# Windowed attention and two expert layers on one core: the first pass of the first layer in the attention's list, q and k in rows of 96 tokens

## The chip, the core and the metric

The kernel runs on one core of one Trainium2 chip, in one launch. The metric is the device time in microseconds (us). The engines are named as in the profile: PE is TensorE (matmul), PEld its weight loads, DVE is VectorE, ACT is ScalarE, POOL is GpSimd, SP is SyncE, which only issues DMAs here.

## What is computed

Attention with a window of 128 tokens over 4 batches, 8 heads, 576 tokens and 64 columns a head; its output, 2304 tokens of 512 columns, goes through two expert layers (512 to 2048 to 512).

```python
rel = pos[:, None] - pos[None, :]
slopes = 2.0 ** (-8.0 * (np.arange(H) + 1) / H)
scores = q @ k.T / np.sqrt(D) + slopes * -abs(rel)      # where 0 <= rel < 128, else -1e9
attn = softmax(scores) @ v                              # sum + 1e-9
x = attn.transpose(0, 2, 1, 3).reshape(B * S, H * D)    # 2304 x 512
h = x @ w_in                                            # first layer
P = a[0] + a[1] * h + a[2] * h**2 + a[3] * h**3
Q = 1.0 + abs(b[0]) * abs(h) + abs(b[1]) * h**2
x = (P / (Q + 1e-6)) @ w_out
h = x @ w2_in                                           # second layer
out = where(h > 0, h, exp(min(h, 0)) - 1) @ w2_out
```

The weights come as 64-bit floats, and the kernel makes 32-bit ones of them on the chip.

## The kernel before

**Attention.** There are 16 units: a batch and a pair of heads. For each unit q, k and v are loaded; q and k come as four tiles of 128 tokens and one of 64 (three DMAs each, the last tile padded with zeros). TensorE transposes them (`qT`, `kT`: five blocks of 128 columns each), ScalarE copies q's (`qC`) and VectorE k's transposes (`kC`) from PSUM, and VectorE the last 64 tokens of both (`zC`). Then come the scores `S` in two halves, nine tiles `t` of 64 queries by up to 192 keys for both heads; VectorE adds the bias and takes the minimum (`D`, L615), ScalarE takes the exponential and the row sums (`E`, L621), VectorE the inverse of the sums in two parts (`R`, L629 and L630: five tiles, then four), GpSimd multiplies the probabilities by it (`N`, L633), TensorE transposes them in four pairs (`T`, L645), ScalarE copies them (`C`, L557), TensorE multiplies by v in two halves (`V`, L675, into the PSUM tiles `evens` and `odds`), and ScalarE copies both results into `xT` (`XE` and `XO`, L557). The probabilities and the raw q, k and v have two sets of buffers each.

**Weights.** A weight tile (there are 32: `wi` and `wo` for 16 blocks of 128 columns of the hidden layer) is loaded as words and takes five steps: scale on ScalarE (`cs`, L279), shift on VectorE (`ca`, L287), join on VectorE (`cb`, L297), high half (`ch`, L305), low half (`cl`, L311). TensorE multiplies halves in three passes: high by high, low by high, high by low.

**First layer.** The 2304 tokens are six blocks `j` of 384. A chunk is a block and one of the 16 hidden blocks `f`: 96 chunks, 16 to a pass. A chunk is GEMM1 (`g`, L402, 12 matmuls into one PSUM bank `h`), the rational function and GEMM2 (`G`, L769, 12 matmuls, added up in four banks over a pass). The rational function has a first part (six operations of ScalarE L445 to L465, three of VectorE) and a second: the high half of the quotient `hi` (L458), the product back (L470), the remainder (L475), and the low half (L476, on VectorE for the first chunks, else on GpSimd).

**What sets the order.** `attention_steps` lists the steps of the attention with engine, cost and needs, `in_time` plays them through with the ranks of the table `OFF`, and `attention` issues them in that order. The list also holds 28 weight conversions, the split of block 0 of x into high and low halves (`xh`, `xl`), GEMM1 of chunks 0 to 3 and the first part of the rational function for chunks 0 and 1. All else is issued by the loop in `experts`: for s from 0 to 95 it issues GEMM1 of chunk s, GEMM2 of chunk s − 3 and `rational(s)`, which is the first part of chunk s and the second part of chunk s − 1; the last four weights are converted on the way (`conv_step`). In the first pass the scale of a weight goes ahead of the GEMMs of every other s. The loop then goes on into the second layer, which is not touched.

Of the kernel before, what the change touches and what calls it, by code (L numbers as in the profile page):

```python
# [41 lines left out]
def attention_steps():  # L42
# [75 lines left out]
    for c in range(4):
        gone = [("S", 14, m) for m in range(2)] if c == 0 else [("S", 15, m) for m in range(2)]
        gone += [("D", 15, t) for t in range(9)] if c == 3 else []  # L120
        step(("xh", c), "ACT", 415, ("XE", 12), ("XO", 12), *gone)
        step(("xl", c), "DVE", 470, ("xh", c))
        bank = {0: ("kC", 15)}.get(c)
        free = [bank] if bank else [("D", 15, t) for t in range(9)]
        for kk in range(4):
            step(("g", c, kk), "PE", 520, ("xl", kk), ("cl", 2 * c), *free, ("g", c, kk - 1),
                 *([("g", c - 1, 3)] if kk == 0 else []))
    for c in range(2):
        gone = [("b_abs",), ("r", c - 1, 3), *[(x, 15, t) for t in range(9) for x in "DN"]]
        step(("r", c, 0), "ACT", 1750, ("g", c, 3), *(gone if c else gone[:2]))  # L130
        step(("r", c, 1), "DVE", 475, ("r", c, 0))
        step(("r", c, 2), "ACT", 900, ("r", c, 1))
# [1213 lines left out]
```

## Time and profile before

| | us |
|---|---|
| median of 3 runs | 939.21 (939.2 to 939.39) |
| profiled execution | 937.85 |
| its span, first to last instruction | 936.1 |
| TensorE busy | 906.1 (97%) |
| VectorE busy | 783.4 (84%) |
| ScalarE busy | 731.6 (78%) |
| GpSimd busy | 178.7 (19%) |

The profile is of one execution. Times are counted from the start of its span, in us; durations of groups are means in ns. "Idle before" is the time an engine stood still ahead of an instruction, and the name behind the arrow is what it waited for. The granted clock (PEclk) is the share of its full speed that the chip let TensorE run at. The stage of the attention ends at about 150 us, the first layer at about 550, the second fills the rest.

### The profile page before, as it was taken

How to read it: one execution, taken by the hardware profiler on the slowest of the kernel's cores; microseconds unless marked ns; L12 is line 12 of the kernel's file. 1: busy time of each engine (PE TensorE's matmuls, PEld its weight loads, DVE VectorE, ACT ScalarE, POOL GpSimd, SP SyncE). 2: the span in 40 equal slices, each digit the busy share in tenths (PEclk: the TensorE clock that was granted, in tenths of full speed). 3: DMA queues.
4: the chain of work that ended last, by engine and by line, in shares of the span. 5: the costliest groups of instructions: out<-in, count | busy, mean ns of one | idle time of the engine just before them, and what ended most of it. 6: DMA issues, size and time to landing. Idle time of an engine off the chain costs nothing.

```text
span 936.1 us, 18028 instructions
## 1 busy us (share of the span) xinstructions
PE 906.1 (97%) x6148; PEld 834.2 (89%) x6148; DVE 783.4 (84%) x1851; ACT 731.6 (78%) x1635; POOL 178.7 (19%) x264
## 2 busy tenths in 40 slices
PE   7989987999999999999999989999999999999998
PEld 4766666999999999999999978898988888888887
DVE  6988997998998998988989979998968688777653
ACT  5999997988898888889888968676867567766553
POOL 4566561122222222222222210000000000000000
PEclk8999998999999999999999989999999999999999
DMA  7999962011222222222200124445243423442201
GB/s 172 220 219 219 242 191 76 1 35 60 83 79 74 87 61 91 85 63 87 84 31 28 46 73 142 150 144 186 92 158 106 124 79 99 150 147 79 80 1 67
DMA packets 112428, 98.43 MB, mean 105 GB/s; under 512 B 62800, under 2 KB 86096, under 8 KB 112336
## 3 DMA queue, kind: packets, MB, share of 16 engines
q1 hardware_dynamic: 109936, 96.70, 34.8%
q8 instruction: 48, 0.79, 0.4%
q10 hardware_dynamic: 2400, 0.59, 0.3%
q14 instruction: 44, 0.36, 0.1%
HBM read 79.96 MB, written 17.30 MB: 104 GB/s over the span
## 4 chain that ended last, share of the span: by engine, by line
PE 76%; DVE 5%; ACT 2%; issue 1%; POOL 0%; DVEq 0%; ACTq 0%
PE acc L993 21%; PE acc L769 19%; PE m L977 19%; PE h L402 18%; DVE ghi L458 1%; DVE ee L479 1%; DVE qq L461 1%; DVE ee L475 1%; DVE qq L470 1%; DVE h L478 0%; ACT rr L464 0%; ACT rr L465 0%; DVE xo_wo L934 0%; DVE xo_wi L934 0%; DVE t_wi L955 0%
## 5 line engine op out<-in xcount | busy, mean ns | idle before, releaser
L402 PE MATMUL h<-xs,w_wi 128*128 128x384 f32 x1152 | 218.3, 336 | 0.0
L402 PEld LDWEIGHTS h<-xs,w_wi 128*128 128x128 f32 x1152 | 201.0, 188 | 0.3
L769 PE MATMUL acc<-ghi,w_wo 128*128 128x384 f32 x768 | 197.3, 338 | 3.0 <-DVE ghi L458 3.0
L476 POOL TENSOR_TENSOR glo<-ee,rr 128x384 fp32r<-128x384 f32 x92 | 93.7, 1018 | 313.3 <-DVE ee L475 106.3
L769 PEld LDWEIGHTS acc<-ghi,w_wo 128*128 128x128 f32 x768 | 140.4, 190 | 3.4 <-DVE ghi L458 3.4
L769 PE MATMUL acc<-glo,w_wo 128*128 128x384 f32 x384 | 129.6, 337 | 0.8 <-DVE glo L476 0.8
L993 PE MATMUL acc<-op_wo,ghi 128*128 128x512 f32 x288 | 89.6, 392 | 0.0
L977 PE MATMUL m<-xo_wi,op_wi 128*128 128x384 f32 x336 | 77.2, 337 | 0.0
L977 PE MATMUL m<-xo_wo,op_wi 128*128 128x384 f32 x336 | 76.5, 335 | 0.2 <-ACT oo L1043 0.2
L769 PEld LDWEIGHTS acc<-glo,w_wo 128*128 128x128 f32 x384 | 73.0, 190 | 1.3 <-DVE glo L476 1.3
L1039 ACT ACTIVATE oo<-qq 128x384 f32<-128x384 f32 x24 | 12.6, 523 | 77.0 <-DVE qq L1033 77.0
L464 ACT ACTIVATE rr<-qq,c_q 128x384 f32<-128x384 f32 x94 | 57.8, 615 | 15.0 <-DVE qq L461 14.2
L447 ACT ACTIVATE oo<-h,a_sb 128x384 f32<-128x384 f32 x94 | 66.4, 706 | 2.3 <-DVE h L478 2.0
L461 DVE SCALAR_TENSOR_TENSOR qq<-h,b_abs,qa 128x384 f32<-128x384 f32 x92 | 56.1, 609 | 14.0 <-ACT qa L446 12.9
L450 ACT ACTIVATE ee<-h,a_sb 128x384 f32<-128x384 f32 x94 | 66.1, 703 | 0.0
L977 PEld LDWEIGHTS m<-xo_wo,op_wi 128*128 128x128 f32 x336 | 60.8, 188 | 4.4 <-ACT oo L1043 0.4
L458 DVE TENSOR_TENSOR ghi<-ee,rr 128x384 fp32r<-128x384 f32 x96 | 53.5, 557 | 12.2 <-ACT h L445 0.5
L993 PEld LDWEIGHTS acc<-op_wo,ghi 128*128 128x128 f32 x288 | 53.5, 188 | 8.9
L479 DVE TENSOR_TENSOR ee<-ee,h 128x384 f32<-128x384 f32 x94 | 52.2, 555 | 10.2 <-DVE h L478 0.5
L977 PEld LDWEIGHTS m<-xo_wi,op_wi 128*128 128x128 f32 x336 | 60.5, 188 | 0.0
L445 ACT ACTIVATE h<-h 128x384 f32<-128x384 f32 x94 | 45.4, 483 | 16.6 <-PE h L402 16.0
L1033 DVE TENSOR_TENSOR ee<-ee,m 128x384 f32<-128x384 f32 x96 | 52.7, 549 | 5.8 <-PE m L977 5.5
(198 smaller groups left out, 2064.4 us busy)
## 6 DMA issues: line engine op xcount, KB each, us to landing
pair<-joined_wo SPq DMA_DIRECT2D x43, 256.0 KB, 2.7
raw_wo<-in_moe_w_out_dram SPq DMA_DIRECT2D x20, 512.0 KB, 4.1
raw_wi<-in_moe_w_in_dram SPq DMA_DIRECT2D x16, 512.0 KB, 4.3
half<-in_moe_w_in_dram SPq DMA_DIRECT2D x32, 256.0 KB, 2.7
two_wo<-joined_wi SPq DMA_DIRECT2D x32, 256.0 KB, 2.8
s<-sums SPq DMA_DIRECT2D x32, 256.0 KB, 2.8
half<-in_moe_w_out_dram SPq DMA_DIRECT2D x22, 256.0 KB, 2.8
v<-in_v_dram SPq DMA_DIRECT2D x32, 128.0 KB, 3.9
```

The costliest lines, as they stand in the source:

```text
L402: nc.tensor.matmul(h, lhsT=WT["wi", f][:, SEL[wp], kk * P:(kk + 1) * P], rhs=x[xp][kk], start=(kk == 0 and n == 0), stop=(kk == KD - 1 and ...
L447: nc.scalar.activation(out=oo, in_=h2, func=AF.Identity, scale=a_sb[:, 3:4], bias=a_sb[:, 1:2])
L450: nc.scalar.activation(out=ee, in_=h2, func=AF.Identity, scale=a_sb[:, 2:3], bias=a_sb[:, 0:1])
L458: nc.vector.tensor_tensor(out=hi, in0=ee0, in1=rr0, op=ALU.mult)
L461: nc.vector.scalar_tensor_tensor(out=qq, in0=h2, scalar=b_abs[:, 1:2], in1=qa, op0=ALU.mult, op1=ALU.add)
L464: nc.scalar.activation(out=rr, in_=qq, func=AF.Ln, bias=c_q)
L476: (nc.gpsimd if c > 4 else nc.vector).tensor_tensor(out=low, in0=ee0, in1=rr0, op=ALU.mult)
L479: nc.vector.tensor_tensor(out=ee, in0=ee, in1=h, op=ALU.add)
L769: nc.tensor.matmul(acc_t[d], lhsT=WT["wo", f][:, SEL[wp], d * P:(d + 1) * P], rhs=gt[SEL[xp]], start=(f == 0 and n == 0), stop=(f == KF - ...
L977: nc.tensor.matmul(out, lhsT=w[:, SEL[wp], c0:c0 + P], rhs=XO[q // NP2, nm, k][:, SEL[xp]], start=(k == 0 and n == 0), stop=(k == 1 and n ...
L993: nc.tensor.matmul(acc_t[T, t], lhsT=gt[SEL[xp]][:, t * P:(t + 1) * P], rhs=w[:, SEL[wp]], start=(first and n == 0), stop=(last and n == 2),)
L1033: nc.vector.tensor_tensor(out=t, in0=R[q, x], in1=M[q, m], op=ALU.add)
```

## The change

The function `attention` becomes `attention_and_first_pass`, and its list of steps now holds the whole first pass: all 32 weights, the split of x for blocks 0 and 1, GEMM1 of all 16 chunks in quarters (`g`), the rational function in single operations (`sq` to `lo`), and GEMM2 of chunks 0 to 12 in quarters (`G`). The loop in `experts` starts at s = 16, and the two first `load_half` stand ahead of it. The first 24 weights are converted as before; the last eight, whose slots hold q, k and the probabilities in the attention, come behind it, with the high half on ScalarE. Three of them wait for G of chunks 0 to 2, whose quotients lie in their slots. From chunk 3 on the low half of the quotient is made by GpSimd.

Beside that, q and k come as six tiles of 96 tokens in two DMAs each, without padding: six transposes of 96 columns, copies `qC` and `kC` of 480 columns, `zC` of two times 96. One `R` per unit inverts all nine sums, behind all nine `E`; every `N` waits for it. The copy `XO` is VectorE's. Costs in the list and the table `OFF` have other numbers.

```diff
-MODE = {"qT": 0, "kT": 0, "T": 0, "S": 1, "V": 2}
+CT = 4160
+MODE = {"qT": 0, "kT": 0, "T": 0, "S": 1, "V": 2, "g": 0, "G": 0}
...
-    "ldq": -37303, "ldk": -40037, "ldv": -7307, "qT": 49228, "qC": -19956, "kT": -37687, "kC":
...
+    "ldq": -23769, "ldk": -74006, "ldv": -1434, "qT": 61759, "qC": -31032, "kT": -8967, "kC":
...
-    for key, cost in (("consts", 1000), ("ident", 700), ("rel", 2100), ("rel_t", 2100)):
+    for key, cost in (("ident", 700), ("rel", 1850), ("rel_t", 1850), ("consts", 500)):
...
-            step(("ld", nm, u), "SP", 1550, (nm + "T", u - 2))
-        step(("ld", "v", u), "SP", 1550, ("V", u - 2, 1))
-        step(("qT", u), "PE", 590, ("ld", "q", u), ("ident",), ("consts",), ("kC", u - 1), ("zC", u - 1))
-        step(("kT", u), "PE", 590, ("ld", "k", u), ("ident",), ("consts",), *([("qC", u)] if u else []))
+            step(("ld", nm, u), "SP", 1150, (nm + "T", u - 2))
+        step(("ld", "v", u), "SP", 1700, ("V", u - 2, 1))
+        step(("qT", u), "PE", 550, ("ld", "q", u), ("ident",), ("kC", u - 1), ("zC", u - 1))
...
-            step(("N", u, t), "POOL", {64: 330, 128: 400, 192: 480}[c], ("R", u, int(t > 4)), ("E", u, t))
-        step(("R", u, 0), "DVE", 320, *[("E", u, t) for t in range(5)])
-        step(("R", u, 1), "DVE", 320, *[("E", u, t) for t in range(5, 9)])
+            step(("N", u, t), "POOL", {64: 380, 128: 480, 192: 600}[c], ("R", u), ("E", u, t))
+        step(("R", u), "DVE", 330, *[("E", u, t) for t in range(9)])
...
-        step(("XO", u), "ACT", 264, ("V", u, 0), ("V", u, 1))
+        step(("XO", u), "DVE", 336, ("V", u, 0), ("V", u, 1))
...
+        gone = [("ldw", n - 1)] if n < EARLY else []
+        if n == 22:
+            gone.append(("bias", 3))
+        if EARLY <= n < EARLY + 3:
+            gone += [("G", n - EARLY, d) for d in range(4)]
+        if n == EARLY + 3:
+            gone.append(("kT", 15))
+        if n >= EARLY + 4:
+            v, x = divmod(n - EARLY - 4, 2)
+            gone += [("T", 14 + v, m) for m in ((0, 1), (2, 3))[x]]
+        step(("ldw", n), "SP", 1300, *gone)
+        step(("cs", n), "ACT", 575, ("ldw", n), ("cl", n - 3), ("cs", n - 1))
+        step(("ca", n), "DVE", 340, ("ldw", n))
+        step(("cb", n), "DVE", 590, ("cs", n), ("ca", n))
+        step(("ch", n), *(("DVE", 337) if n < EARLY else ("ACT", 520)), ("cb", n))
+        step(("cl", n), "DVE", 610, ("ch", n))
+    step(("small",), "SP", 300)
+    step(("b_abs",), "ACT", 60, ("small",))
+    over = [("C", 15, m) for m in range(4)] + [("XE", 15), ("XO", 15)]
+    banks = [[(x, 15, t) for x in "D" for t in range(9)]] * 3 + [[("kC", 15), ("qC", 15)]]
...
+    for c in range(16):
+        bank = (3, 0, 1, 2)[c] if c < 4 else (3, 0, 1)[(c - 4) % 3]
+        gone, banks[bank] = banks[bank], [("hm", c)]
+        for kk in range(4):
+            step(("g", c, kk), "PE", 520, ("xl", 0, kk), ("cl", 2 * c), *gone, ("g", c, kk - 1), ("g", c - 1, 3))
+        start = [(x, 15, t) for x in "DN" for t in range(9)] if c == 1 else []
+        step(("sq", c), "ACT", 389, ("g", c, 3), ("oo", c - 1), ("ee", c - 1), ("qq", c - 1), *start)
...
+        gone = [(("qT", 14),), (("qT", 15),), (("kT", 14),), (*over, ("V", 15, 1))][min(c, 3)]
+        step(("hi", c), "DVE", 475, ("ex", c), ("ea", c), *gone, ("G", c - 3, 3))
+        step(("q2", c), "DVE", 588, ("hi", c))
+        step(("e2", c), "DVE", 475, ("q2", c))
+        step(("lo", c), *(("POOL", 1050) if c > 2 else ("DVE", 475)), ("e2", c))
+        for d in range(4 if c < 13 else 0):
+            step(("G", c, d), "PE", 520, ("hi", c), ("lo", c), ("cl", 2 * c + 1), ("G", c, d - 1), ("G", c - 1, 3),
+                 *(over if c == 0 else []))
...
-        if eng == "D":
+        if key in LATE:
+            nc.scalar.activation(out=w[:, 0], in_=T32[key], func=AF.Copy)
+        else:
             nc.vector.tensor_copy(w[:, 0], T32[key])
...
+    def low_quotient(c):
+        _, ee, _, _, rr = r_t.pop(c)
+        (nc.gpsimd if c > 2 else nc.vector).tensor_tensor(out=g_t[c][1], in0=ee, in1=rr, op=ALU.mult)
...
-            shape = [P, NF + 1, 2, D]
+            R6 = S // 6
             whole = {
-                nm: [place(LATE["qk".index(nm) * 2 + n], shape, F32, nm) for n in range(2)] for nm in "qk"
+                nm: [place(LATE["qk".index(nm) * 2 + n], [P, 6, 2, D], F32, nm) for n in range(2)] for nm in "qk"
             }
-            whole["v"] = [raw.tile(shape, F32, name=f"v{n}") for n in range(2)]
+            whole["v"] = [raw.tile([P, NF + 1, 2, D], F32, name=f"v{n}") for n in range(2)]
             units = [(b, p) for p in range(NP) for b in range(B)]
...
-                    eng.dma_start(
-                        out=t[:, 0:NF, e, :],
-                        in_=src[b, 2 * p + e, 0:NF * P, :].rearrange("(t p) d -> p t d", p=P),
-                    )
-                eng.dma_start(
-                    out=t[0:TL, NF, :, :], in_=src[b, 2 * p:2 * p + 2, NF * P:S, :].rearrange("h p d -> p h d")
-                )
+                    if nm == "v":
+                        eng.dma_start(
+                            out=t[:, 0:NF, e], in_=src[e, 0:NF * P].rearrange("(t p) d -> p t d", p=P)
+                        )
+                    else:
+                        eng.dma_start(out=t[0:R6, :, e], in_=src[e].rearrange("(t p) d -> p t d", p=R6))
+                if nm == "v":
+                    eng.dma_start(out=t[0:TL, NF], in_=src[:, NF * P:S].rearrange("h p d -> p h d"))
...
-                    tp_ps[u, n] = ps = bank(1 if (u, n) == (0, 1) else 7, [P, NF, P], "ps_qk")
-                    for i in range(NF + 1):
+                    tp_ps[u, n] = ps = bank(1 if (u, n) == (0, 1) else 7, [P, 5, R6], "ps_qk")
+                    for i in range(6):
                         nc.tensor.transpose(
-                            ps[:, i] if i < NF else odds[:, NF + 2 * n:NF + 2 * n + 2].rearrange("p t c -> p (t c)"),
-                            r[:, i].rearrange("p e d -> p (e d)"), ident,
+                            ps[:, i] if i < 5 else ends[:, n], r[0:R6, i].rearrange("p e d -> p (e d)"),
+                            ident[0:R6, 0:R6],
                         )
                 return run
 
             def q_copy(n, eng):
...
-            def inverse(u, half):
-                t0, t1 = ((0, 5), (5, 9))[half]
-                total = stat(u, 1, t0, t1)
+            def inverse(u):
+                total = stat(u, 1, 0, 9)
                 nc.vector.tensor_scalar(out=total, in0=total, scalar1=1e-9, scalar2=None, op0=ALU.add)
-                nc.vector.reciprocal(out=stat(u, 2, t0, t1), in_=total)
+                nc.vector.reciprocal(out=stat(u, 2, 0, 9), in_=total)
 
...
-                    copy("ACT", x[:, n::2], odds[:, 0:NF] if n else x_t.pop(u))
+                    copy("DVE" if n else "ACT", x[:, n::2], odds[:, 0:NF] if n else x_t.pop(u))
...
-        for s in range(NCH):
+        _, ee, qq, _, rr = r_t.pop(KF - 1)
+        q_t[KF - 1] = (qq, ee, rr)
+        load_half(0)
+        load_half(1)
+        for s in range(KF, NCH):
             o = s - SK
             j, f = divmod(s, KF)
-            if j == 0 and f % 2 and f > 2:
-                conv_step(to_conv, later=True)
-            if s >= 4:
-                run_all(gemm1(s, f, x1[j], (7, 4, 5)[(s - 4) % 3]))
+            run_all(gemm1(s, f, x1[j], (7, 4, 5)[(s - 4) % 3]))
             if f == KF - 1 and j + 1 < NB:
                 x1[j + 1] = split_x(j + 1, at_home, nc.vector)
-            if o >= 0:
-                gemm2_T(o)
+            run_all(gemm2_T(o))
             if joins(s):
                 rational(s, beside=(lambda: join_shift(nj), lambda: join_words(nj), lambda: keep_half(nj)))
                 nj += 1
             elif s >= LAST:
                 prepare(s)
             else:
-                rational(s, beside=(go_on, go_on, go_on))
-            if s == KF - 2:
-                load_half(0)
-                load_half(1)
+                rational(s)
```

The rational function's operations are those of before, one small function each; `rational` itself serves chunks from 16 on.

**End of the attention, TensorE.** `odds` and `evens` are V of the last unit, `h` is GEMM1, `acc` is GEMM2. Before:

```order
L675 MATMUL odds<-pT,v_93 64x64 x2
L675 MATMUL evens<-pT,v_93 64x64 x2
L402 MATMUL h<-xs_2437,w_wi_930 128x384 x3
L769 MATMUL acc<-ghi_2715,w_wo_447 128x384 x2
L769 MATMUL acc<-glo_2716,w_wo_447 128x384
```

After:

```order
L717 MATMUL odds<-pT,v_93 64x64 x2
L717 MATMUL evens<-pT,v_93 64x64 x2
L386 MATMUL h<-xs_2373,w_wi_851 128x384 x3
L386 MATMUL h<-xs_2430,w_wi_851 128x384 x3
L463 MATMUL acc<-g_wi_2529,w_wo_422 128x384 x3
L386 MATMUL h<-xs_2273,w_wi_1017 128x384 x3
L463 MATMUL acc<-g_wi_2529,w_wo_422 128x384 x3
L386 MATMUL h<-xs_2273,w_wi_1017 128x384 x2
L386 MATMUL h<-xs_2373,w_wi_1017 128x384
L463 MATMUL acc<-g_wi_2529,w_wo_422 128x384 x3
```

Before, one quarter of GEMM1 of chunk 3 stands behind V and then all of GEMM2 of chunk 0; after, half of chunk 3 stands there, and then quarters of GEMM2 of chunk 0 and of GEMM1 of chunk 4 in turn.

**End of the attention, VectorE.** `ghi` and `g_wi` take the quotient of chunk 0: L458 or L440 is its high half, L476 or L454 its low half; L297, L305, L311 are weight conversions. Before:

```order
L305 CAST w_wi_2668<-cvt_2639 128x512
L287 TENSOR_SCALAR raw_wo_2614<-raw_wo_2614 128x512
L311 TENSOR_TENSOR w_wi_2668<-cvt_2639,w_wi_2668 128x512
L297 SCALAR_TENSOR_TENSOR cvt_2673<-cvt_2673,raw_wo_2614 128x512
L305 CAST w_wo_2697<-cvt_2673 128x512
L311 TENSOR_TENSOR w_wo_2697<-cvt_2673,w_wo_2697 128x512
L458 TENSOR_TENSOR ghi_2715<-ee_2520,rr_2523 128x384
L470 SCALAR_TENSOR_TENSOR qq_2521<-qq_2521,ghi_2715 128x384
L475 TENSOR_TENSOR ee_2520<-ee_2520,qq_2521 128x384
L476 TENSOR_TENSOR glo_2716<-ee_2520,rr_2523 128x384
```

After:

```order
L440 TENSOR_TENSOR g_wi_2529<-ee_2457,rr_2460 128x384
L307 TENSOR_SCALAR raw_wo_2479<-raw_wo_2479 128x512
L444 SCALAR_TENSOR_TENSOR qq_2458<-qq_2458,g_wi_2529 128x384
L450 TENSOR_TENSOR ee_2457<-ee_2457,qq_2458 128x384
L602 COPY xT<-odds 128x4x64
L414 SCALAR_TENSOR_TENSOR qq_2558<-h_2556,b_abs,qq_2558 128x384
L454 TENSOR_TENSOR g_wi_2529<-ee_2457,rr_2460 128x384
```

Before, the quotient of chunk 0 comes behind the last conversion of the attention's list. After, it lies around the odds copy of unit 14 (L602); that of unit 15 stands ten rows further down.

**One unit in the attention, GpSimd.** Each row is `N` of one or more tiles by number of columns. Before:

```order
L633 TENSOR_SCALAR pr_wi_101<-pr_wi_101,qq_100 128x128
L633 TENSOR_SCALAR pr_wi_101<-pr_wi_101,qq_100 128x64
L633 TENSOR_SCALAR pr_wi_101<-pr_wi_101,qq_100 128x192
L633 TENSOR_SCALAR pr_wo_102<-pr_wo_102,qq_100 128x192
L633 TENSOR_SCALAR pr_wi_101<-pr_wi_101,qq_100 128x192 x2
L633 TENSOR_SCALAR pr_wo_102<-pr_wo_102,qq_100 128x192 x3
L633 TENSOR_SCALAR pr_wi_103<-pr_wi_103,qq_100 128x128
L633 TENSOR_SCALAR pr_wi_103<-pr_wi_103,qq_100 128x64
```

After:

```order
L675 TENSOR_SCALAR pr_wi_101<-pr_wi_101,qq_100 128x64
L675 TENSOR_SCALAR pr_wo_102<-pr_wo_102,qq_100 128x192
L675 TENSOR_SCALAR pr_wi_101<-pr_wi_101,qq_100 128x192 x2
L675 TENSOR_SCALAR pr_wi_101<-pr_wi_101,qq_100 128x128
L675 TENSOR_SCALAR pr_wi_101<-pr_wi_101,qq_100 128x192
L675 TENSOR_SCALAR pr_wo_102<-pr_wo_102,qq_100 128x192 x3
L675 TENSOR_SCALAR pr_wi_103<-pr_wi_103,qq_100 128x64
```

The nine `N` of a unit come in another order; 128 and 64 columns are tiles 1 and 0, and `pr_wo` holds the third and fourth pair.

## Rows read from the trace of the kernel before

**Rows 1.** Windows: start:end, length, busy us by engine, PEclk, DMA share, GB/s
```profile
0.00:20.00 20.00, 14.33 (x94) 9.12 (x94) 12.72 (x56) 9.12 (x30) 8.71 (x36) 0.83 0.81 164
20.00:140.00 120.00, 108.42 (x1797) 83.45 (x1796) 106.99 (x452) 113.48 (x396) 72.59 (x131) 0.99 0.87 218
140.00:150.00 10.00, 9.01 (x131) 7.10 (x129) 5.30 (x10) 9.05 (x20) 3.77 (x7) 1.00 0.60 191
150.00:160.00 10.00, 6.20 (x19) 5.37 (x20) 9.55 (x20) 6.16 (x13) 0.00 (x0) 0.66 0.00 1
160.00:200.00 40.00, 40.00 (x233) 40.00 (x232) 37.24 (x73) 35.38 (x66) 8.16 (x8) 1.00 0.03 8
...
160.00:480.00 320.00, 320.00 (x1848) 320.00 (x1847) 287.85 (x602) 283.77 (x559) 76.37 (x75) 1.00 0.21 67
```

**Rows 2.** Chain that ended last, behind 155 us: start, us, what
```profile
155.52 3.57 PE acc L769 x10
...
209.43 2.08 PE h L402 x12
```

**Rows 3.** Timeline of PE: start, us, instruction, [idle before, what ended it]
```profile
149.76 0.23 PE L675 MATMUL evens<-pT,v 64*64 64x64 f32 x2
149.92 0.79 PE L402 MATMUL h<-xs,w_wi 128*128 128x384 f32 x3
153.74 1.01 PE L769 MATMUL acc<-ghi,w_wo 128*128 128x384 f32 x2 [3.03 <-DVE ghi L458]
155.52 0.69 PE L769 MATMUL acc<-glo,w_wo 128*128 128x384 f32 x1 [0.77 <-DVE glo L476]
```

**Rows 4.** The costliest groups, page: busy us, mean ns, idle before
```profile
L458 DVE TENSOR_TENSOR ghi<-ee,rr 128x384 fp32r<-128x384 f32 x96 | 53.5, 557 | 12.2 <-ACT h L445 0.5
```

**Rows 5.** Timeline of DVE, around 61 us
```profile
61.00 0.17 DVE L629 TENSOR_SCALAR qq<-qq 128x5 f32<-128x5 f32 x1
...
61.31 0.32 DVE L615 CUSTOM_DVE_ANT_0 pr_wo<-s_ps,bias_even 128x192 f32<-128x192 f32 x1
...
61.55 0.69 DVE L297 SCALAR_TENSOR_TENSOR cvt<-cvt,raw_wi 128x512 int32<-128x512 int32 x1
```

**Rows 6.** Groups by line and form of DVE, 20 to 120 us
```profile
L559 DVE COPY qkT<-ps_qk 128x512 f32<-128x512 f32 x14 | 9.6, 685 | 0.4 <-PE ps_qk L581 0.4
...
L297 DVE SCALAR_TENSOR_TENSOR cvt<-cvt,raw_wo 128x512 int32<-128x512 int32 x10 | 7.1, 710 | 1.1 <-ACT cvt L279 1.1
...
L287 DVE TENSOR_SCALAR raw_wo<-raw_wo 128x512 int32<-128x512 int32 x10 | 5.1, 514 | 2.4 <-DMA raw_wo<-in_moe_w_out_dram 2.1
...
L559 DVE COPY qkT<-odds 128x128 f32<-128x128 f32 x14 | 3.9, 278 | 1.9 <-PE evens L675 1.1 <-PE odds L675 0.8
```

**Rows 7.** Timeline of ACT: odds copy, scale of a weight, one chunk
```profile
62.77 0.38 ACT L557 ACTIVATE xT<-odds 128x256 f32<-128x256 f32 x1
63.04 0.46 ACT L621 ACTIVATE pr_wo<-pr_wo,qq 128x192 f32<-128x192 f32 x1
...
65.59 0.68 ACT L279 ACTIVATE cvt<-raw_wo 128x512 f32<-128x512 f32 x1
...
158.22 0.47 ACT L445 ACTIVATE h<-h 128x384 f32<-128x384 f32 x1
...
161.62 0.49 ACT L445 ACTIVATE h<-h 128x384 f32<-128x384 f32 x1
```

**Rows 8.** Tile xT: ns min/median/max, first and last start us
```profile
L557 ACT ACTIVATE xT<-odds x16: 357/378/421, 30.0 to 150.4; 128x256 f32<-128x256 f32 x16
```

**Rows 9.** Groups by line and form of PE, 20 to 120 us
```profile
L581 PE MATMUL ps_qk<-ident,k_wo 128*128 128x128 f32 x28 | 4.4, 281 | 0.0
```

**Rows 10.** Groups by line and form of POOL, 20 to 120 us
```profile
L633 POOL TENSOR_SCALAR pr_wo<-pr_wo,qq 128x192 f32<-128x192 f32 x50 | 29.5, 604 | 16.7 <-DVE qq L630 7.6 <-PE s_ps L608 4.1 <-PE evens L675 3.5
```

**Rows 11.** DMA issues to 160 us: count, KB each, median us to landing
```profile
q_wi<-in_q_dram SPq DMA_DIRECT2D x16, 128.0 KB, 3.6
...
q_wi<-in_q_dram SPq DMA_DIRECT2D x8, 32.0 KB, 3.5
```

More of the change, by code (lines that the diff above doesn't have):

```diff
@@ L118, in attention_steps @@
[L118 to L132, printed above, removed]
-        step(("r", c, 3), "DVE", 1000, ("r", c, 0), ("r", c, 1))
+        gone = [("ldw", n - 1)] if n < EARLY else []
[3 more added lines that the diff above has]
+            gone += [("G", n - EARLY, d) for d in range(4)]
@@ L410, in run_all, with squared, with_abs @@
             pass
-    def rational_new(c):
-        h = h_t.pop(c)
-        h2, ee, qq, oo, rr = [row(t) for t in ("h2", f"ee{c}", f"qq{c}", "oo", f"rr{c}")]
-        nc.scalar.activation(out=h2, in_=h, func=AF.Square)
-        nc.scalar.activation(out=qq, in_=h, func=AF.Abs, scale=b_abs[:, 0:1])
+    def squared(c):
+        r_t[c] = [row(t) for t in ("h2", f"ee{c % 2}", f"qq{c % 2}", "oo", f"rr{c % 2}")]
+        nc.scalar.activation(out=r_t[c][0], in_=h_t[c], func=AF.Square)
+    def with_abs(c):
+        part[c] = qa = bank(6, [P, TB], "qa") if c > 3 else r_t[c][2]
+        nc.scalar.activation(out=qa, in_=h_t[c], func=AF.Abs, scale=b_abs[:, 0:1])
@@ L422, in rational_new, with log, inverse_below @@
         )
-        yield
-        nc.scalar.activation(out=rr, in_=qq, func=AF.Ln, bias=c_q)
-        nc.scalar.activation(out=rr, in_=rr, func=AF.Exp, scale=-1.0)
-        q_t[c] = (qq, ee, rr)
-        yield
-        nc.vector.tensor_tensor(out=h, in0=oo, in1=h, op=ALU.mult)
-        nc.vector.tensor_tensor(out=ee, in0=ee, in1=h, op=ALU.add)
-        yield
+    def log(c):
+        nc.scalar.activation(out=r_t[c][4], in_=r_t[c][2], func=AF.Ln, bias=c_q)
+    def inverse_below(c):
+        nc.scalar.activation(out=r_t[c][4], in_=r_t[c][4], func=AF.Exp, scale=-1.0)
@@ new lines, in times_h, with above, quotient @@
+    def times_h(c):
+        nc.vector.tensor_tensor(out=h_t[c], in0=r_t[c][3], in1=h_t[c], op=ALU.mult)
+    def above(c):
+        nc.vector.tensor_tensor(out=r_t[c][1], in0=r_t[c][1], in1=h_t.pop(c), op=ALU.add)
+    def quotient(c):
+        if c < 3:
+            t = place(LATE[c], [P, 2, TB], F32R, "g")
+            g_t[c] = (t[:, 0], t[:, 1])
+        else:
+            if not tmp:
+                opener.pop()()
+                tmp.append(ctx.enter_context(tc.tile_pool(name="tmp", bufs=1)))
+            g_t[c] = (row(f"ghi{c % 3}", F32R), row(f"glo{c % 3}", F32R))
+        _, ee, _, _, rr = r_t[c]
+        nc.vector.tensor_tensor(out=g_t[c][0], in0=ee, in1=rr, op=ALU.mult)
@@ new lines, in back, with remainder, gemm2_T @@
+    def back(c):
+        qq = r_t[c][2]
+        nc.vector.scalar_tensor_tensor(
+            out=qq, in0=qq, scalar=EPSC, in1=g_t[c][0].bitcast(F32), op0=ALU.add, op1=ALU.mult
+        )
+    def remainder(c):
+        _, ee, qq, _, _ = r_t[c]
+        nc.vector.tensor_tensor(out=ee, in0=ee, in1=qq, op=ALU.subtract)
+    def low_quotient(c):
+        _, ee, _, _, rr = r_t.pop(c)
+        (nc.gpsimd if c > 2 else nc.vector).tensor_tensor(out=g_t[c][1], in0=ee, in1=rr, op=ALU.mult)
+    def gemm2_T(c):
+        j, f = divmod(c, KF)
+        gt = g_t.pop(c)
+        for d in range(KD):
+            if f == 0:
+                acc_t[d] = bank(d, [P, TB], "acc")
+            for n, (wp, xp) in enumerate(PASS):
+                nc.tensor.matmul(
+                    acc_t[d], lhsT=WT["wo", f][:, SEL[wp], d * P:(d + 1) * P], rhs=gt[SEL[xp]],
+                    start=(f == 0 and n == 0), stop=(f == KF - 1 and n == 2),
+                )
+            yield
+        if f == KF - 1:
+            for d in range(KD):
+                nc.scalar.activation(out=xT[:, d, j * TB:(j + 1) * TB], in_=acc_t[d], func=AF.Copy)
@@ L475, in rational @@
             nc.vector.tensor_tensor(out=ee0, in0=ee0, in1=qq0, op=ALU.subtract)
-            (nc.gpsimd if c > 4 else nc.vector).tensor_tensor(out=low, in0=ee0, in1=rr0, op=ALU.mult)
+            nc.gpsimd.tensor_tensor(out=low, in0=ee0, in1=rr0, op=ALU.mult)
         if new:
@@ L553, in attention @@
             odds = bank(2, [P, 2 * NF, Q], "odds")
+            ends = odds.rearrange("p t c -> p (t c)")[:, NF * Q:NF * Q + 2 * R6].rearrange("p (n c) -> p n c", c=R6)
             def copy(eng, out, in_):
@@ L1313 @@
     with tc.manual_schedule():
-        attention()
+        attention_and_first_pass()
         experts()
```

186 lines of the change are left out of this document (70 added, 116 removed), and 20 rows, old and new, of the table OFF.

## The prediction

> **What bounds the kernel now.** I read the busy time by stage first, then the chain that ends last, then the engines' own time around 150 us. [...] So behind the attention TensorE sets the time, and the end lies at a fixed distance from one moment: the start of GEMM1 of chunk 16, the first chunk of the second pass, at 209.43 [rows 2], from which both kernels run the same loop. What the change is worth is by how much that moment moves.
>
> Ahead of it there are two stages. In the attention (to about 150) no engine is full: between 20 and 140 ScalarE is busy for 113.5 of 120 us, TensorE for 108.4, VectorE for 107.0, GpSimd for 72.6 [rows 1]. At its end there is a hole: V's last matmul ends at 149.99, a quarter of g3 follows, then TensorE idles for 3.03 us (the reader should see the releaser, VectorE's hi half of chunk 0), then for 0.77 us for the low half [rows 3]. The granted clock is 0.66 of full from 150 to 160 [rows 1], and the first G takes 3.57 us, where a group later takes 2.08 [rows 2]. The clock fell in the stretch in which TensorE stood idle.
>
> **Term 1, behind the attention.** Before: from 149.99 to 209.43 are 59.4 us. The work in it is a quarter of g3 (0.52) and 25 groups, g4 to g15 and G0 to G12, of 2.08: 52.5 us; 6.9 us are lost to the hole and to the lower clock. After: in VectorE's new row the hi half, the product back, the remainder and the low half of chunk 0 stand ahead of the last unit's odds copy, so G0 can begin as soon as the PSUM banks of the attention are free, and TensorE's row has quarters of g3, G0 and g4 in turn right after V's last. That is half of g3 (1.04) and the same 25 groups: 53.0 us.
>
> Are the others quick enough for it? VectorE has, behind the last odds copy and up to the low half of x for chunk 16, 78 operations on rows of 384 columns. One busies it for 0.557 [rows 4]; a long operation begins about 0.08 before the one ahead of it ends (61.31 + 0.32 against 61.55) [rows 5], so it takes 0.48 where it waits for nothing and up to 0.55 where it follows from the one ahead. With it comes the rest of eight late weights: 4 shifts, 8 joins, 7 low halves, by the means [rows 6] less 0.08, the low half as the join: 4 × 0.43 + 15 × 0.63 = 11. That is 48.5 to 54 us in a stretch of 54.6 (the low half of x is wanted in GEMM1's last quarter). ScalarE's chunk takes 3.40 (158.22 to 161.62) [rows 7]; 13 chunks are 44, about one of them behind the moment, eight weights add 0.57 and about 0.5 for scale and high copy (8.5): 49 to 51. So VectorE is at 89 to 99% and ScalarE at about 93%, beside 93 and 88% from 160 to 200 [rows 1], where TensorE lost nothing. The new stage is tighter than any that the trace shows with TensorE full; I take 1.2 us of stall, nearer to the trace's nothing than to the upper bound of 4 us, which is the hole of now come back (3.03 + 0.77). Term 1 is 59.4 − 53.0 − 1.2 = **5.2 us gained** (2.4 to 6.4).
>
> **Term 2, the attention up to V's last.** ScalarE: the 16 odds copies leave it (one a unit, 30.0 to 150.4, so a unit takes 8.03 us [rows 8]), 0.27 us each from start to start (62.77 to 63.04) [rows 7], −4.3; four weights fewer are scaled there, 0.68 less the same overlap of 0.11 [rows 7], −2.3; the first half of one chunk more, +3.4. That is −3.2, and about −0.4 for q's copy of 480 columns instead of 512. VectorE: the odds copy of 256 columns has no row there; it lies between 128 columns (0.278) and 512 (0.685) [rows 6], by the line between them 0.41 less the overlap, 0.33 each, +5.3 (4 to 9.6 at the two ends). One pair of small operations fewer per unit, 0.31 from start to start (61.00 to 61.31) [rows 5], −4.8 or so; the two other copies +0.6. Ten rational operations more, +5.4. Conversions ahead of the last copy: one shift more, three joins, two high copies and two low halves fewer, by the means [rows 6] less overlap (a high copy as a shift), −3.6. Sum +2.9. TensorE: 12 transposes of 96 columns for 10 of 128 per unit; at 0.157 us each (4.4 by 28) [rows 9] that is −2.5 in all if the cost goes by columns and +5.0 if it goes by instructions; and a quarter of g fewer, −0.5.
>
> Busy time to 150 then goes for ScalarE from 131.7 to 128.1, for VectorE from 125.0 to 127.9, for TensorE from 131.8 to something between 128.8 and 136.3 (sums of the first three rows of [rows 1]). With the idle time of now (18.3, 25.0 and 18.2) they would end at 146.4, 152.9 and 147.0 to 154.5. VectorE's idle time is mostly others' lateness, and ScalarE is the one with the least idle time between 20 and 140, so I keep near it and take 148: **2.0 us gained** (from 4.5 lost, TensorE's upper end, to 7.3 gained, if ScalarE's work falls by 3.6 and half of its 7.4 idle us behind the first 20 go too).
>
> The edits at nothing: the first 20 us hardly change (the planes come ahead of the constants, and no row of mine starts earlier than its data); the activation of b sits elsewhere on ScalarE, 0.2 us; the two first half loads of the second layer are issued after chunk 15 and not behind chunk 14's work, with the DMA share at 0.03 there [rows 1]; the low half on GpSimd from chunk 3 on takes about 1 us of an engine that is busy for 8 of 40 us there [rows 1].
>
> **Sum.** 937.85 − 5.2 − 2.0 = 930.65 for the profiled execution. The median of the runs lies 1.36 above that execution, so 932.0.
>
> **Rivals.**
> R1, slower: one inverse per unit. Today five of a unit's nine N on GpSimd can start on the first sums; now all nine wait for the last exponential. They take up to 0.604 each [rows 10], so T gets its data up to 3.0 us later. Two sets of probabilities hide that latency as long as the next unit's scores keep the others busy; GpSimd's 8 us a unit hold 5.4 us of N. Against it: 16.7 us of GpSimd's idle time ended at the 50 N of the second buffer, 7.6 for the sums [rows 10], so it has room. If T is 1 us later per unit in earnest, 16 units lose 16: 937.85 − 5.2 − 2.0 + 16 + 1.36 = 948.0. It decides from 7.2 / 16 = 0.45 us a unit. Chance 0.06.
> R2: VectorE (or TensorE by its 12 transposes) becomes the bound of the attention, end at 152.9: 937.85 − 5.2 + 2.9 + 1.36 = 936.9. For it: +2.9 on an engine with 107 of 120 busy. Chance 0.13.
> R3: the tail is tighter than priced, and VectorE's late weights push G's back by 4 us: 934.8. Chance 0.19.
> R4: term 2 comes in full (7.3): 937.85 − 5.2 − 7.3 + 1.36 = 926.7. Chance 0.14.
> R5, the change does not do what it says: G0 still stands still for a half that comes late, by a lagging VectorE, and the clock falls again; the attention's 2.0 alone remain: 937.2. Chance 0.05.
> R6: the loads of q and k. They are a third of what a unit moves (576 KB of about 1,750), and the DMA share of 0.87 [rows 1] makes 7.0 us of a unit's 8.03; with six rows on each of 96 partitions for 4.5 on 128 they could take up to 4/3 as long, 7.8 of 8.0 us if all else stood still (7.0 + 2.3 × 1/3). Then term 2 is gone, and VectorE's waits for weights, 2.1 us at ten `raw_wo` in 100 us [rows 6], would come twice over for both kinds: 2 × 2.1 × 1.2 = 5.0 lost, 939.0. Against it stands that a load of 64 partitions with 32 KB landed after 3.5 and one of 128 with 128 KB after 3.6 us [rows 11], so a load's time here is not set by its partitions. Chance 0.03.
>
> [...]
>
> **How the numbers follow.** Forecast 0.40, R3 0.19, R4 0.14, R2 0.13, R1 0.06, R5 0.05, R6 0.03. About 0.2% (1.9 us) is what a measurement of this kernel can tell from no change, so faster means under 937.3. Forecast, R3, R4, most of R2 and half of R5 lie there: 0.85. The rest of R2 and R5, and R6, are within it: 0.09. R1: 0.06. The extremes of both terms together give 925.5 to 941.3; 926.5 to 938.0 leaves out half of R4, R1 and R6, under 0.2.
>
> **What would show it.** Term 1: after V's last matmul no idle time over 1 us on TensorE, a granted clock near 1.0 in the 10 us behind it, and 53 to 55 us from V's end to chunk 16's g. R3 would show as TensorE waiting for VectorE's hi or remainder in that stretch, and VectorE over 97% busy. Term 2: V's last near 148 and chunk 16's g near 202.2. R1 would show as TensorE waiting for N in the transposes well over today's few us, R2 as VectorE over 92% busy between 20 and 140, R6 as the shift waiting for weights and a DMA share over 0.93. If V's last comes after 152, term 2 was wrong; if the clock falls at the seam, term 1 was.

## The result, and the profile after

The changed kernel takes 944.45 us in the median (941.84 to 947.91), the kernel before 938.59 in the same runs (937.16 to 939.39): a ratio of 1.0066, 95% interval 1.0043 to 1.0088. It is slower, where 932.0 and a gain were forecast. The profiled execution took 945.33 us, its span is 943.6, 7.5 more than before.

The windows of the changed kernel (start:end, length, busy us of PE, PEld, DVE, ACT, POOL, granted clock, DMA share, GB/s) answer [rows 1]:

```profile
0.00:20.00 20.00, 14.15 (x90) 8.96 (x94) 12.53 (x47) 7.65 (x24) 4.89 (x25) 0.95 1.02 184
...
0.00:161.30 161.30, 137.41 (x2047) 104.25 (x2047) 126.24 (x503) 128.93 (x430) 76.26 (x168) 0.94 0.83 184
...
20.00:140.00 120.00, 102.88 (x1683) 79.16 (x1675) 96.37 (x406) 100.83 (x351) 61.91 (x126) 0.92 0.87 193
...
150.00:160.00 10.00, 10.00 (x140) 8.68 (x137) 8.05 (x16) 9.23 (x21) 2.77 (x7) 1.00 0.64 188
...
161.00:216.00 55.00, 54.16 (x325) 53.77 (x322) 53.67 (x100) 49.58 (x96) 12.62 (x10) 1.00 0.11 35
```

From 20 to 140 every engine does less: ScalarE 100.8 us for 113.5, VectorE 96.4 for 107.0, TensorE 102.9 for 108.4. TensorE's granted clock is 0.92 there, 0.99 before. The DMA engines are as busy as before (0.87), but they move 193 GB/s where they moved 218. Behind the attention TensorE is as good as full and VectorE is busy for 53.7 of 55 us. The row to 161.30 is the whole attention, up to V's last matmul.

The seam, on the timeline of PE (start, us, instruction), answers [rows 3]:

```profile
161.07 0.23 PE L717 MATMUL evens<-pT,v 64*64 64x64 f32 x2
161.23 1.31 PE L386 MATMUL h<-xs,w_wi 128*128 128x384 f32 x6
162.38 0.68 PE L463 MATMUL acc<-g_wi,w_wo 128*128 128x384 f32 x3
162.90 0.68 PE L386 MATMUL h<-xs,w_wi 128*128 128x384 f32 x3
...
215.50 2.24 PE L386 MATMUL h<-xs,w_wi 128*128 128x384 f32 x12
```

V's last matmul ends at 161.30, GEMM1 and GEMM2 follow in turn without a hole, and chunk 16's GEMM1 begins at 215.50. So the stage behind the attention takes 54.2 us (59.4 before), and the attention ends 11.3 us later than at 149.99. That is 11.3 − 5.2 = 6.1 of the 7.5 us by which the span grew; 0.6 more is a wait of G13 in the loop for the low half that GpSimd makes, and the last 0.8 were not followed.

What the engines stood idle for between 20 and 150 us (engine, line, what was waited for: us in total, times, longest), changed kernel:

```profile
PEld ps_qk L624 <- issue: 11.4, 6, 3.0
PE ps_qk L624 <- issue: 9.7, 5, 2.8
...
DVE raw_wo L307 <- DMA raw_wo<-in_moe_w_out_dram: 8.1, 6, 3.0
ACT cvt L299 <- DMA raw_wo<-in_moe_w_out_dram: 6.3, 6, 2.4
DVE raw_wi L307 <- DMA raw_wi<-in_moe_w_in_dram: 6.0, 5, 2.6
ACT cvt L299 <- DMA raw_wi<-in_moe_w_in_dram: 3.7, 5, 1.9
```

And the kernel before in the same stretch:

```profile
DVE raw_wo L287 <- DMA raw_wo<-in_moe_w_out_dram: 2.1, 2, 1.5
DVE raw_wi L287 <- DMA raw_wi<-in_moe_w_in_dram: 1.8, 2, 1.2
ACT cvt L279 <- DMA raw_wo<-in_moe_w_out_dram: 1.4, 3, 0.6
...
PEld ps_qk L581 <- issue: 1.1, 4, 0.3
...
ACT cvt L279 <- DMA raw_wi<-in_moe_w_in_dram: 0.2, 1, 0.2
```

VectorE waits 14.1 us for weight words (3.9 before), ScalarE 10.0 (1.6), both mostly at the same moment, with all that stands behind the conversion in their rows. Two such places, from the timelines of SP and DVE:

```profile
62.41 0.50 SPq L286 DMA_DIRECT2D raw_wo<-in_moe_w_out_dram  x1
...
80.87 0.50 SPq L281 DMA_DIRECT2D raw_wi<-in_moe_w_in_dram  x1
```

```profile
68.47 0.43 DVE L307 TENSOR_SCALAR raw_wo<-raw_wo 128x512 int32<-128x512 int32 x1 [2.96 <-DMA raw_wo<-in_moe_w_out_dram]
...
85.89 0.73 DVE L307 TENSOR_SCALAR raw_wi<-raw_wi 128x512 int32<-128x512 int32 x1 [1.22 <-DMA raw_wi<-in_moe_w_in_dram]
```

In both places the words are used the moment they land, 6.1 and 5.0 us behind the issue of their load. So short a distance is not new: from 24 to 106 us the kernel before uses each weight 4.0 to 5.9 us behind its issue, but there the loads are issued 4.2 to 6.0 us apart and have mostly landed (medians of 4.3 and 4.4 us to 160 us). From 20 to 116 us the changed kernel issues them 1.6 to 8.5 us apart, often two close together (62.41 and 63.98, the next at 72.44); they land after medians of 4.9 and 5.1, and each is used 4.2 to 8.7 us behind its issue, waits included.

TensorE also waits, 9.7 us at the transposes of q, for what the profile calls issue. The timelines show what it is: each of these five waits ends 0.1 us behind VectorE's copy of k's transposes, which the list demands beforehand, and each of these copies begins 0.6 to 1.3 us behind the start of a conversion that stood at its words. The place at 68.47 again:

```profile
69.42 0.65 DVE L602 COPY qkT<-ps_qk 128x480 f32<-128x480 f32 x1
...
70.17 1.03 PE L624 MATMUL ps_qk<-ident,q_wo 96*128 96x96 f32 x5 [2.84 <-issue]
```

The chain of work that ended last, from 20 to 161 us, goes through five such loads, 27.8 us in sum (start, us):

```profile
38.26 5.38 DMA raw_wo<-in_moe_w_out_dram
...
47.98 6.95 DMA raw_wo<-in_moe_w_out_dram
...
80.87 4.99 DMA raw_wi<-in_moe_w_in_dram
...
98.40 5.06 DMA raw_wo<-in_moe_w_out_dram
...
115.80 5.40 DMA raw_wi<-in_moe_w_in_dram
```

The load itself stands in SyncE's row behind loads of v, and those wait for V of two units before: 27.2 us in sum from 10 to 145, 16.5 before (waits of SP's queue, changed kernel, then before):

```profile
SPq L545 <- PE evens L717: 27.2, 8, 7.9
```

```profile
SPq L503 <- PE evens L675: 16.5, 7, 6.8
```

### The profile page after: what moved, and what is told of

It reads as the page before. It is cut to its first block, busy times and chain, and to the rows that moved or that the text cites. A ratio compares the mean times of both kernels' runs of the same rounds, so it can differ in the third digit from the quotient of the medians.

```text
span 943.6 us, 18030 instructions
## 1 busy us (share of the span) xinstructions
PE 910.6 (96%) x6180; PEld 837.8 (89%) x6180; DVE 784.3 (83%) x1830; ACT 728.9 (77%) x1623; POOL 174.5 (18%) x261
## 4 chain that ended last, share of the span: by engine, by line
PE 87%; DVE 4%; DMA 4%; ACT 2%; issue 1%; POOL 1%; SPq 0%; POOLq 0%; DVEq 0%; ACTq 0%
PE acc L1003 21%; PE acc L463 21%; PE h L386 21%; PE m L987 19%; DMA raw_wo<-in_moe_w_out_dram 2%; PE s_ps L651 2%; PE ps_pT L687 1%; DMA raw_wi<-in_moe_w_in_dram 1%; PE ps_qk L624 1%; PE odds L717 1%; PE evens L717 1%; DVE qkT L602 1%; DMA b_raw<-in_moe_b_dram 1%; POOL pr_wi L675 0%; DVE cvt L317 0%
## 5 line engine op out<-in xcount | busy, mean ns | idle before, releaser
L386 PE MATMUL h<-xs,w_wi 128*128 128x384 f32 x1152 | 224.5, 336 | 0.7 <-ACT xs L744 0.4
L463 PE MATMUL acc<-ghi,w_wo 128*128 128x384 f32 x744 | 190.0, 336 | 0.0
L516 POOL TENSOR_TENSOR glo<-ee,rr 128x384 fp32r<-128x384 f32 x81 | 82.4, 1017 | 253.9 <-DVE ee L515 103.0
L501 DVE SCALAR_TENSOR_TENSOR qq<-h,b_abs,qa 128x384 f32<-128x384 f32 x80 | 48.7, 609 | 12.6 <-ACT qa L486 11.6
L504 ACT ACTIVATE rr<-qq,c_q 128x384 f32<-128x384 f32 x80 | 49.2, 615 | 12.2 <-DVE qq L501 11.6
L487 ACT ACTIVATE oo<-h,a_sb 128x384 f32<-128x384 f32 x80 | 56.5, 707 | 1.8 <-DVE h L518 1.6
L1003 PE MATMUL acc<-op_wo,glo 128*128 128x512 f32 x144 | 57.0, 396 | 0.0
L490 ACT ACTIVATE ee<-h,a_sb 128x384 f32<-128x384 f32 x80 | 56.3, 703 | 0.0
L498 DVE TENSOR_TENSOR ghi<-ee,rr 128x384 fp32r<-128x384 f32 x81 | 45.7, 564 | 10.6 <-ACT h L485 0.5
L675 POOL TENSOR_SCALAR pr_wi<-pr_wi,qq 128x192 f32<-128x192 f32 (+2 forms) x80 | 40.5, 520 | 75.6 <-DVE qq L672 25.8
```

The source lines that it names most:

```text
L386: nc.tensor.matmul(h, lhsT=WT["wi", f][:, SEL[wp], kk * P:(kk + 1) * P], rhs=x[xp][kk], start=(kk == 0 and n == 0), stop=(kk == KD - 1 and ...
L463: nc.tensor.matmul(acc_t[d], lhsT=WT["wo", f][:, SEL[wp], d * P:(d + 1) * P], rhs=gt[SEL[xp]], start=(f == 0 and n == 0), stop=(f == KF - ...
L487: nc.scalar.activation(out=oo, in_=h2, func=AF.Identity, scale=a_sb[:, 3:4], bias=a_sb[:, 1:2])
L490: nc.scalar.activation(out=ee, in_=h2, func=AF.Identity, scale=a_sb[:, 2:3], bias=a_sb[:, 0:1])
L498: nc.vector.tensor_tensor(out=hi, in0=ee0, in1=rr0, op=ALU.mult)
L501: nc.vector.scalar_tensor_tensor(out=qq, in0=h2, scalar=b_abs[:, 1:2], in1=qa, op0=ALU.mult, op1=ALU.add)
```

## The experiments

All are compared with the kernel before on the same chip; its median in each set stands beside it. Four suspects were set against each other: the form of q and k (A), the order as a whole (B), the start (C), and the words that come late in that order (D).

**Rows of 128 in the changed kernel.** Its own order; only loads, transposes and copies of q and k as before, with the padding written by VectorE.

```diff
-                        eng.dma_start(out=t[0:R6, :, e], in_=src[e].rearrange("(t p) d -> p t d", p=R6))
+                    eng.dma_start(
+                        out=t[:, 0:NF, e], in_=src[e, 0:NF * P].rearrange("(t p) d -> p t d", p=P)
+                    )
+                eng.dma_start(out=t[0:TL, NF], in_=src[:, NF * P:S].rearrange("h p d -> p h d"))
```

> The changed kernel in its own order, but q and k in rows of 128 as before (three loads, padded last tile, transposes of 128 columns). Theory A (a load on 96 partitions costs more of the DMA engines: q1 took 4.49 us of 16 engines' time per MB to 160 us after, 3.99 before): V's last comes from 161.3 back to 150 to 155, q1 back to about 4.0 us per MB, 934 to 938 us. Theory B (the order asks for loads too late or blocks engines, whatever their form): V's last stays within 2 us of 161.3, 942 to 946.

Measured: 943.64 us (before 939.37), ratio 1.0058 (1.0030 to 1.0086), not to be told from the changed kernel. V's last ends at 160.0, so the time and V's last are theory B's. SyncE's waits for V at the loads of v fall to 17.0 us (from 10 to 145, 16.5 before), yet VectorE and ScalarE still wait 13.1 and 9.8 us for words.

**Rows of 96 in the kernel before**, the same edit the other way round:

> The kernel before in its own order, with q and k in rows of 96 alone (two loads, six transposes of 96 columns, no pads). Theory A: q1 at about 4.5 us per MB and V's last 4 to 10 us later than 150.0, 942 to 948. Theory B: within 2 us of the kernel before, 936 to 940.

Measured: 943.01 (before 939.37), ratio 1.0038 (1.0015 to 1.0060): alone they cost 3.6 us, in theory A's range, though V's last comes only 2.9 us later (152.9). The queue q1 up to 160 us (packets, MB, share of 16 engines), changed kernel, the same with rows of 128, the kernel before with rows of 96, and the kernel before:

```profile
q1 hardware_dynamic: 64504, 28.62, 80.4%
```

```profile
q1 hardware_dynamic: 65040, 28.78, 71.3%
```

```profile
q1 hardware_dynamic: 65760, 30.36, 82.4%
```

```profile
q1 hardware_dynamic: 66240, 30.36, 75.8%
```

So rows of 96 do cost transfer time, 6.6% of 160 us there and 9.1% in the changed order. Bytes of q and k are 9.4 MB, which at before's 4.0 us per MB are 38 us: the 10.6 and 14.6 us on top are an estimate of 28 and 39%, around the third that R6 names. But in the changed order the time taken back bought nothing. A is true, and by itself it does not explain the 11.3 us.

**The activation of b later.** In the changed kernel it stands ahead of the first q copy on ScalarE, and holds it for a load of 1 KB:

```profile
9.09 0.20 ACT L775 ACTIVATE b_abs<-b_raw 128x2 f32<-128x2 f32 x1 [5.93 <-DMA b_raw<-in_moe_b_dram]
9.20 0.55 ACT L600 ACTIVATE qkT<-ps_qk 128x480 f32<-128x480 f32 x1
```

```diff
+                if name == "b_abs":
+                    continue
+                if (name, *args) == ("xh", 0, 0):
+                    RUN["b_abs"]()
```

> The changed kernel, but the activation that makes b_abs stands on ScalarE ahead of the first split of x instead of ahead of the first q copy, which it held up to 9.29 us (b landed at 9.07). Theory A: the first unit starts 2 us earlier, but the loads set the pace: 942 to 945. Theory C (the start is lost by b_abs and all later units only carry it on): V's last 2 to 5 us earlier, 939 to 942.

> Both edits at once: rows of 128 and a late b_abs, in the changed kernel's order. Theory A with C: V's last at 148 to 152, 931 to 936, faster than the kernel before by the seam's 5 us. Theory B: 940 to 944.

Measured: 945.20 and 944.50 (before 939.37), V's last at 164.7 and 159.3. With rows of 128 the edit starts the first q copy 1.1 us earlier (7.84 for 8.95) and leaves the first exponential at 11.97. Neither run is faster: C falls, and with A's edit beside it the loss stays, as theory B has it.

**Words one weight earlier.** The changed kernel's order, but the load of weight n + 1 stands where that of n stood; the load of weight 22 stands behind the bias planes at the start.

```diff
+                if name == "ldw" and args[0] < EARLY - 1:
+                    if args[0] == 0:
+                        load_w(order[0])
+                    if args[0] + 1 != 22:
+                        load_w(order[args[0] + 1])
+                    continue
```

> The changed kernel in its own order, but each of the first 24 weights is loaded one weight earlier on SyncE's queue (the load of weight n+1 stands where that of n stood). Theory D (VectorE and ScalarE stand still in order at conversions whose words have not landed: 14.1 and 10.0 us from 20 to 150 us, 3.9 and 1.4 before): these waits fall under 3 us, V's last comes from 161.3 to 152 to 156, 936 to 939 us. Theory E (the queue is short anyway, and a weight that comes earlier makes q, k and v come later): V's last within 2 us of 161.3, TensorE's waits at the transposes of q and k grow past 12 us, 943 to 947.

> Weights one place earlier and q and k in rows of 128, in the changed kernel's order. Theory D with A (each transfer dearer by 96 partitions: q1's share to 160 us fell from 80 to 71% with rows of 128): V's last at 149 to 153, 931 to 936. Theory E: 941 to 945.

Measured: 935.82 and 932.83 (before 938.72), ratios 0.9967 (0.9943 to 0.9991) and 0.9937 (0.9916 to 0.9957). The first is 8.6 us under the 944.45 of the changed kernel, and its V's last ends at 154.1, in theory D's range. TensorE's waits called issue at the transposes, 9.7 us, are gone, where theory E had them grow. But the waits for words did not fall under 3 us, as D had it; they are 8.3 us on VectorE and 7.7 on ScalarE (20 to 150):

```profile
DVE raw_wi L307 <- DMA raw_wi<-in_moe_w_in_dram: 5.5, 4, 2.4
ACT cvt L299 <- DMA raw_wi<-in_moe_w_in_dram: 5.5, 3, 2.5
...
DVE raw_wo L307 <- DMA raw_wo<-in_moe_w_out_dram: 2.8, 3, 1.3
...
ACT cvt L299 <- DMA raw_wo<-in_moe_w_out_dram: 2.2, 2, 1.4
```

With rows of 128 beside it they do fall, and V's last ends at 148.9. With the words early the rows of 128 are worth 3.0 us (runs of 931.12 to 934.22 against 934.02 to 938.16), about as much as in the kernel before. So D comes first and A counts behind it: in V's last of the profiled executions, rows of 128 gave 1.3 us without the early words and 5.1 with them. Windows of the one with rows of 96, then of that with rows of 128:

```profile
20.00:140.00 120.00, 108.08 (x1786) 82.14 (x1786) 104.34 (x437) 106.61 (x377) 65.83 (x133) 0.99 1.01 194
```

```profile
20.00:140.00 120.00, 110.23 (x1813) 83.81 (x1814) 107.10 (x443) 111.98 (x389) 74.13 (x144) 0.97 0.82 203
```

With 96 partitions the DMA engines are full (1.01) at 194 GB/s, with 128 they have room (0.82) at 203. The waits for words from 20 to 150 in the latter:

```profile
ACT cvt L299 <- DMA raw_wi<-in_moe_w_in_dram: 1.7, 1, 1.7
DVE raw_wi L307 <- DMA raw_wi<-in_moe_w_in_dram: 1.5, 2, 1.3
DVE raw_wo L307 <- DMA raw_wo<-in_moe_w_out_dram: 0.7, 1, 0.7
```

**The same in the kernel before**, as a control (weight 22 in turn here and below):

> The kernel before in its own order, each weight after the first loaded one weight earlier on SyncE's queue. If the late words are a fault of the changed list (theory D), there is little to take here (VectorE's and ScalarE's waits for words were 3.9 and 1.4 us): 936 to 940. If earlier weights help any order by as much as they helped the changed one (8.6 us): 930 to 933.

Measured: 937.03 (before 937.68), ratio 0.9998 (0.9975 to 1.0021). The same edit gains nothing here, so what it mends is a fault of the changed list.

**The list made anew with the loads' old costs.**

```diff
-            step(("ld", nm, u), "SP", 1150, (nm + "T", u - 2))
-        step(("ld", "v", u), "SP", 1700, ("V", u - 2, 1))
+            step(("ld", nm, u), "SP", 1550, (nm + "T", u - 2))
+        step(("ld", "v", u), "SP", 1550, ("V", u - 2, 1))
...
-        step(("ldw", n), "SP", 1300, *gone)
+        step(("ldw", n), "SP", 1550, *gone)
```

> The changed kernel, its list made anew with the loads' costs of before (1550 each, in place of 1150 for q and k, 1700 for v and 1300 for weights), all else as changed. Theory D (the list asks for words and tokens before they land, since it prices loads too low): waits for loads fall by half, V's last at 152 to 157, 936 to 941. If the order of the other steps is what costs: 942 to 946.

Measured: 966.26 (before 938.72), ratio 1.0295. Both expectations missed. Its waits for words from 20 to 150 grew instead:

```profile
ACT cvt L299 <- DMA raw_wi<-in_moe_w_in_dram: 16.2, 4, 5.9
DVE raw_wi L307 <- DMA raw_wi<-in_moe_w_in_dram: 11.8, 3, 4.8
```

The old prices with the new table make a worse order, and say nothing on whether the new prices are too low. That the table `OFF` goes with the costs it was made with is a reading of this, not shown.

**The odds copy.** On VectorE in the kernel before, and back on ScalarE in the changed one (rows of 128, words early):

```diff
-                    copy("ACT", x[:, n::2], odds[:, 0:NF] if n else x_t.pop(u))
+                    copy("DVE" if n else "ACT", x[:, n::2], odds[:, 0:NF] if n else x_t.pop(u))
```

> The kernel before in its own order, with the odds copy on VectorE alone. By my prices ScalarE gains 4.3 us and VectorE pays 5.3 up to 150; with VectorE's idle time as cover V's last moves by -1 to +2 and the time by as much: 937 to 941. If VectorE is the bound of the attention: 942 or more.

> Rows of 128, weights one place earlier, and the odds copy back on ScalarE in the same place of the order. If the move to VectorE is worth what I priced (ScalarE 4.3 us lighter, VectorE 5.3 heavier, near balance): within 2 us of 932.8. If ScalarE is the bound of the attention: 935 to 937; if VectorE is: 929 to 931.

Measured: 941.12 (before 938.72), 0.1 above its range but with a ratio of 1.0014 (0.9996 to 1.0033), and 931.28 (before 937.68), ratio 0.9919 (0.9893 to 0.9945) beside 0.9937 without it. By these runs the move gains nothing; what it costs, if anything, is under their resolution. The 931.28 also shows that the gain of the early words does not hang on weight 22 at the start, since here it is loaded in turn.

**How far it goes.** Words two places early, and words one place early with the late activation of b, both with rows of 128:

> The changed kernel's order, q and k in rows of 128, weights two places earlier instead of one. Theory D: what is left of the waits for words (2.2 us on VectorE, 1.7 on ScalarE) goes, at the price of later q, k and v at the start: 931 to 934. If the start's loads decide: 934 to 938.

> Rows of 128, weights one place earlier, and b_abs ahead of the first split of x. With the words in time the 2 us that b_abs holds ScalarE at the start are no longer hidden by later waits: 930 to 932. If the start is made good by the slack of later units: 932 to 934.

Measured: 932.07 and 930.26 (before 937.68), ratios 0.9934 (0.9913 to 0.9955) and 0.9915 (0.9888 to 0.9943). Both are in the first of their two ranges. The second is the fastest kernel here, 7.4 us under the kernel before, though its interval overlaps the others of its kind. In its profile V's last ends at 146.1 and chunk 16's GEMM1 begins 53.9 us behind it:

```profile
20.00:140.00 120.00, 112.07 (x1841) 85.22 (x1837) 107.74 (x444) 114.50 (x395) 75.20 (x144) 0.98 0.83 207
```

```profile
145.90 0.23 PE L714 MATMUL evens<-pT,v 64*64 64x64 f32 x2
146.06 1.31 PE L386 MATMUL h<-xs,w_wi 128*128 128x384 f32 x6
...
200.03 2.24 PE L386 MATMUL h<-xs,w_wi 128*128 128x384 f32 x12
```

ScalarE is at 114.5 of 120 us there, as full as in the kernel before.

## Why the prediction was wrong

**Term 1 was right.** 54.2 us were forecast from V's last to chunk 16's GEMM1 (53.0 of work, 1.2 of stall), 54.2 came (161.30 to 215.50). That it fits to the tenth is luck, since the stall was chosen between nothing and 4 us. The hole is gone and the clock stayed at 1.00. From 161 to 216 VectorE was busy for 97.6%, over the 97% named as a sign of R3, and its price of 48.5 to 54 us was sound. But R3 did not come, nor did R5: the one wait of TensorE for another engine there, 0.8 us, was for the low half of a quotient on GpSimd, an edit that was put at nothing, and not for VectorE.

**Term 2 failed, and at one step**: "With the idle time of now" the engines "would end at 146.4, 152.9", and 148 was taken. The busy times up to V's last were about right: ScalarE 128.9 us (128.1 forecast), VectorE 126.2 (127.9), TensorE 137.4 (128.8 to 136.3). What was wrong is that idle time was carried over from another order: up to 161.30 ScalarE stood idle for 32.4 us and not 18.3, VectorE for 35.1 and not 25.0, TensorE for 23.9 and not 18.2. In the new order conversions come up before their words have landed, and the copies and transposes that follow them wait too. I took the idle time of before for a property of the work and did not lay SyncE's new row beside the conversions that need it; words of weights that come late appear in the prediction only under R6, as an effect of the rows of 96. With the words earlier V's last came 7.2 us sooner (154.1), and with rows of 128 beside it 12.4 us (148.9), more than the 11.3 that were lost. That this kernel, at 932.83, comes close to the forecast 932.0 does not bear the forecast out: it is another kernel.

**R6 had the right place and the wrong price.** It named the shift waiting for words, with 5.0 us lost; the waits rose by 10.2 us on VectorE and 8.4 on ScalarE. Its other sign, a DMA share over 0.93, did not come from 20 to 140 (0.87). Its cause, the dearer rows of 96, is real but gives 3.0 to 3.6 us, and only where words do not already hold the engines. I argued it down to 0.03 with landing times of single loads (3.5 and 3.6 us) [rows 11]. That row was no evidence: the time on the DMA engines, which q1's share shows, rose all the same, by an estimated 28% in the kernel before (82.4% against 75.8% for the same bytes) and 39% in the changed order. The third in R6, six rows for 4.5, was an estimate by the count of rows; that the time goes by that count was not shown.

**The edits at nothing.** The activation of b was priced at 0.2 us. ScalarE stood still for 5.93 us at the start for it, until 9.09, and the first q copy began at 9.20, where it began at 7.19 before. Moved behind alone it gave nothing; with words in time and rows of 128 the runs are 932.83 as it was and 930.26 with it moved, ratios 0.9937 and 0.9915, whose intervals overlap. The two are of different sets, and weight 22 is loaded at another place, so the 2.6 us are not shown to be its price. That the "first 20 us hardly change" was wrong too: the DMA share rose from 0.81 to 1.02 there, and ScalarE was busy for 7.65 us and not 9.12.

**R1 and R2 did not come.** R1: PEld's waits for N ahead of the transposes T fell from 4.8 to 2.1 us between 20 and 120, and VectorE was busy for 96.4 of 120 us, less than before. One inverse a unit was not tried by itself, since the order of the N hangs on it; what it is worth stays open. So does how the loss parts between SyncE's row that stands at v and a list that asks for words too soon; moving the weights ahead mends both. The run with rows of 128 alone speaks against the first as the main part: SyncE waited hardly longer for V there than before (17.0 and 16.5 us), and the words came late all the same.
